# Score matmuls in blocks of 32 queries, and every loaded quad's probabilities turned by VectorE

## The chip, the cores and the metric

The kernel runs on one core of one Trainium2 chip. The metric is the device time of one execution in microseconds; the median of three runs of the kernel before is 609.25 us (608.87 to 609.41). TensorE has two clock levels, 1.2 and 2.4 GHz; in the profiled execution the granted clock is 1.00, that is 2.4 GHz, in every stretch.

## The reference

Attention over a window of fewer than 16 positions on either side, joined with one summary for each block of 32 positions, feeds a two-layer feed-forward part. Shapes: batch 4, 8 heads, 768 positions, 64 features a head; 3072 tokens of 512 features, hidden size 2048.

```
k_sum = k.reshape(B, H, 24, 32, D).max(axis=3)          # 24 summaries a sequence
v_sum = v.reshape(B, H, 24, 32, D).mean(axis=3)
scores_l = where(|i - j| < 16, q @ k.T / 8, -1e9)
scores_s = q @ k_sum.T / 8 + log(32)
a = softmax(concat([scores_l, scores_s]))               # divided by (sum + 1e-9)
x = (a @ concat([v, v_sum])) -> (3072, 512)
h = x @ w_in;  g = h * erf(softplus(h));  out = g @ w_out
```

## The kernel before

The tokens are worked in six chunks of 512 (NCH). Attention is worked in *quads*: one chunk for one pair of heads, four pairs, so 24 quads numbered 0 to 23. The feed-forward part is worked in 24 steps k, each a chunk and a quarter g of the hidden size. Step k computes h for its quarter (up to step 7 by `mm1`, L829; from step 8 by a scheme with seven products instead of eight, `products`, L870 to L879), applies softplus and erf on ScalarE, multiplies and splits the result into a high and a low part (`gsplit`, L971 to L983), and adds it into the output banks with three matmuls for one (`mm2`, L1000; the first two steps in one float32 matmul, L996).

Quads 0 to 3 are a special start: whole keys are loaded, masks are added by TensorE (L537), and scores go against windows of 96 keys and 24 summaries apart (L546). Quads 4 to 23 are *loaded* quads. `load_quad` loads 64 queries at a time against a window of 96 keys made on the host (`k_win`, 480 KB a quad); a copy puts the 24 key summaries behind each window (L259). `scores` (L546) makes, for each block of 64 queries and either head, one 64 x 64 matmul with 120 columns (96 keys, 24 summaries), into the PSUM banks pA and pB. A float32 matmul is recorded twice, so a quad has 32 records. `softmax` then adds the mask on VectorE (L637), takes the maximum (L642), has eight exponentials on ScalarE (L652) and normalizes on VectorE (L668).

The value product `av` (L711) wants the probabilities with keys on the partitions. There are two ways. Quads 4 to 11 are turned by TensorE: `transp` (L682) makes eight 128 x 120 transposes into pA and pB, and ScalarE copies the two banks into the tile ptr (L688). Quads 12 to 23 (DQ = 12) are turned by VectorE: `turn_blocks` transposes every 32 x 32 block of the 1024 columns (L569) into the tile tb, and sixteen moves of 32 x 256 or 24 x 256 (L259, by VectorE or ScalarE) bring the blocks to the right partitions of ptr. There is one tile for the probabilities (pr) and one for the turned ones (ptr).

All operations are put into a plan with what they read and write. The list ORDER names them by number in the order in which they are issued; a letter behind the number (d, a) gives VectorE or ScalarE where either can do it. Each engine works its own operations in this order, and all loads are issued from one queue (SP). Activation tables are loaded where the order of ScalarE's operations needs another one (L1269). Fixed numbers of idle matmuls fill TensorE's waits at the start (L1039). Weights are loaded and split into high and low parts on VectorE and ScalarE in the first 110 us; sums of weights for the later scheme are made in steps 5 to 7.

Of the kernel before, what the change touches and what calls it, by code (L numbers as in the profile page):

```python
# [25 lines left out]
NP = H // 2  # L26
# [7 lines left out]
NK = LW + NS  # L34
NCH = B * S // T
# [14 lines left out]
0 1 8 3 2 4 9 5 51 11 18 19 35 14 20 21 28 22 29 23 10 30 66 12 67 24 31 6 34 36 32 13 50 37 68 25 38 26 39 44 7 40 69 27d 225 70 45 33d 46 41 71 42  # L50
226 43d 105 72 47 48 107 49d 106a 52 108a 74 78 93d 94a 95 53 112 96 15 73 114 60 97 54 109 149 61 55 56 98 75 77 110a 16 113a 111 76 79 115a 57 62 17
58 59d 80 121 81 151 227a 123 63 174 82 64 87 83 116 65d 122 88 117d 89 119 84 118 173 125 99d 124a 130 100d 126a 251 90 101 132 152 91 102 133 85 92d
103 127 86d 104 136 128a 150 134 137a 120 129 135a 131 178 154a 153d 221 138 155 228a 141 139a 156 142 140 207 159a 144 160d 157 161 145 162 143 179a
158 146 163 229 243 165d 180a 166d 164 181 148 147 244 259 215 216 185 167 210 245 211 168 258 212 209 213 175 217 246 214d 247 218 182d 267 183d 219d
271 252 169d 170d 232 177 184 171 233 222 234 172 235 187d 220 264 248 189 230 249 186 188d 223 237 250 238 190 239 194d 191 240 231 176 265 193a 192
280 269 208 236a 320 254 224 273 241d 262 321 260d 195 275 261a 242 196 266 270 309 197 199d 253 200d 279 201 281 198 325 268 202 341 326 340 272 306
274 308 278 327 277 255 276 328 263 329 382 346 386 203d 204d 385 205 389 282d 330 284 256 310 257 331 206 288a 311 332 283a 307 312 290 314 313a 285
315 294a 336 342a 316 286 358 289d 344 343d 291 322 287 295a 292 317 333 323d 390 359 296 324 394 318a 337 300a 393 319 293 345 397 297 363 302 298
338 347 364 378 379 339 348 301a 374 400a 349 398 350 303 334 352 365 384 401d 304 375 353 354 366 351a 416 380a 355 367 335 299 388 392 356d 412 402
396 305 383 403 376 387 413 406a 368 407d 404 391 369 408 377 370 395 381a 357 360 405 424 361d 371 414 399 425 409 426 362 417d 427 430 418 410 419  # L60
411 431 420 372 449 421 415 422 450d 482 423a 451 481 428a 485 373 429 435 484 436 446 497 447 452 453 437 483 438 487 503 439 488 489 454 448d 432
# [12 lines left out]
875 892d 827a 927 826a 824d 828a 893 900 819a 818a 925 838 901a 897a 898 907a 823d 879 902 908 903a 904 909 914 905a 910 915 916 911 978 912 917d 920
932 913 979 981 918 957d 968 958d 961 971 919d 959 922 960 964 921 929 993 931 926 933 966 962 982 965 972 980 930 994d 934 970 973 996 974 969 975
935 995 936 976 987d 999 1082 997d 1001 988 1000d 1003 998 967a 1004 989a 937 1002d 1005 990 938 985d 1007 1006a 939 986 1009 1008a 983d 1011 1010a
940 984 1013 1012a 1015 1014 944a 950d 1017 942a 946d 1083 947a 948d 1019 943d 951a 1018 956a 954d 1021 952a 1084 1020 1023 992 1016 1027 955d 991
1024d 1022d 1028 1026 945d 949d 1029 941d 1025 953d 1030 1031 1087 1032 1033 1034 1086 1093 1035 1085 1036 1090 1037 1038 1070 1071 1066 1075 1063a
1073 1062d 1067 1039 1076 1077 1065 1040 1078 1069 1041 1079 1091d 1089 1080 1064 1092 1081 1096 1181 1094d 1072a 1098 1042 1095 1097a 1100 1074 1043
1101 1068 1099a 1102 1044 1088 1104 1103a 1045 1106 1105a 1108 1107a 1051d 1049a 1110 1047d 1109a 1057d 1059a 1060d 1112 1052a 1111 1046d 1048a 1114  # L80
1061d 1182 1053a 1055d 1054a 1116 1056d 1115 1058a 1113 1118 1183 1117 1120 1119a 1166 1122 1124 1050d 1125 1187 1126 1121a 1127 1185 1128 1129 1130
1123 1189 1131 1132 1184 1190d 1133 1191 1186 1134 1168 1135 1169 1164 1174 1172 1160 1165 1175 1161a 1136 1176 1159 1177 1137 1162 1138 1178 1163
1192 1179 1180 1167 1195 1281 1193d 1197 1188 1196a 1170a 1139 1194 1199 1173 1200 1265 1198a 1201 1140 1171d 1287 1203 1141 1202a 1205 1204a 1142
1207 1206a 1209 1208a 1148d 1150a 1147d 1211 1153a 1210 1156d 1144a 1213 1155d 1282 1152a 1157d 1291 1215 1149d 1214 1143a 1146d 1217 1283 1212 1219
1158d 1218d 1223 1292 1221 1372 1224 1285 1225 1145d 1216 1226 1154d 1227 1220d 1151d 1222 1228 1297 1229 1230 1231 1298d 1284 1286 1232 1299 1233
1268 1234 1267 1263 1274 1260a 1271 1258 1264 1235 1275 1289 1276 1261 1277 1236 1262 1237 1278 1259 1290 1279 1300 1280 1303 1269d 1388 1301d 1305
1270d 1304a 1302 1293 1307 1295 1272 1308 1294 1306a 1296 1309 1238 1266 1311 1310a 1313 1239 1288 1240 1312a 1315 1314a 1241 1317 1316a 1273 1319
1318 1247a 1321 1256d 1389 1320 1323 1322 1251d 1325 1255d 1390 1324 1327 1326d 1248d 1331 1329 1328d 1250d 1332 1242d 1330 1245d 1333 1244d 1254d
1392 1334 1253d 1252d 1257d 1335 1243d 1249d 1336 1246d 1337 1393 1402 1338 1339 1405 1391 1403a 1340 1404 1341 1374 1375 1342 1370 1381 1367a 1378
1371 1382 1368 1343 1383 1384 1366d 1344 1373 1345 1385 1386 1369 1396d 1387 1398d 1397 1408 1406d 1491 1399 1410 1376d 1409a 1407 1394a 1412 1377a  # L90
1379 1346 1413 1400d 1411a 1395 1347 1414 1401 1348 1416 1415a 1349 1418 1417a 1420 1419a 1353d 1364a 1422 1357d 1421a 1356d 1355a 1361d 1424 1365a
1423 1358d 1354a 1426 1380 1350d 1363a 1352d 1492 1360a 1428 1359d 1427 1351a 1425 1430 1493 1429 1432 1431a 1362d 1434 1436 1433d 1437 1438 1435 1439
1440 1495 1441 1442 1443 1496 1497 1444 1494 1445 1500 1498a 1446 1477 1447 1478 1475 1484 1481 1476 1471d 1485 1448 1486 1474 1487 1449 1472d 1450
1499 1488 1489 1473 1490 1503 1501d 1584 1505 1479a 1451 1504a 1502 1480a 1507 1482 1452 1508 1506a 1453 1509 1454 1511 1510a 1513 1512a 1470d 1459a
1515 1461d 1514a 1467d 1463a 1468d 1517 1460a 1516d 1483 1456d 1457a 1519 1518 1458a 1465a 1521 1520 1585 1462a 1523 1469a 1522 1464a 1525 1455a 1524
# [70 lines left out]
def block_attention_mlp(ctx: ExitStack, tc: tile.TileContext, q_t, k_nat, k_win, v_tok, v_nat, v_win, w_in, w_out, out):  # L166
# [42 lines left out]
    for m in (mask_h, mask_sb):  # L209
        nc.scalar.copy(m, band.unsqueeze(1).to_broadcast([128, 7, NK]))  # L210
# [1101 lines left out]
```

## Time and profile before

| | |
|---|---|
| Median of three runs | 609.25 us |
| The profiled execution, its span | 609.45 us, 607.7 us |
| TensorE matmuls, weight loads | 601.8 us (99%), 500.7 us (82%) |
| VectorE, ScalarE, GpSimd | 472.3 us (78%), 457.6 us (75%), 4.7 us (1%) |
| Moved by the queues | 153.35 MB, 252 GB/s in the mean |

The span runs from the first to the last instruction; the rest of the execution's time lies around it. Busy time is the time in which an engine has an instruction under way. Matmuls overlap: the next begins before the one ahead has ended, so the time that one costs is read from start to start, not from its duration.

### The profile page before, as it was taken

Reading aid. Unit: us, or ns where it says so; the run is one execution under the profiler, and the core shown is the slowest. Engines: PE = TensorE matmul, PEld = TensorE weight load, DVE = VectorE, ACT = ScalarE, POOL = GpSimd, SP = SyncE. Lnnn points to the kernel's source line nnn. Section 1 sums busy time; section 2 is a strip of 40 time slices with the busy share of each in tenths; the row PEclk is TensorE's granted clock in tenths of the full one; section 3 lists DMA queues with packets and bytes.
Section 4 is the critical chain, followed back from the end, with each engine's and each line's share of the span. In section 5 each row is a group of like instructions: output and inputs, shape, how many; then the busy total and the mean of one; then the engine's idle time right before and its main releaser. Section 6 shows DMA issues by size and latency. Waiting matters only on the chain.

```text
span 607.7 us, 11862 instructions
## 1 busy us (share of the span) xinstructions
PE 601.8 (99%) x4624; PEld 500.7 (82%) x4624; DVE 472.3 (78%) x810; ACT 457.6 (75%) x925; POOL 4.7 (1%) x29
## 2 busy tenths in 40 slices
PE   9999999999999999999999999999999999999997
PEld 4677476888888889889889889899898898888886
DVE  4899899757799999979799968669778677546452
ACT  5879799866969798977987787887886884652550
POOL 3000000000000000000000000000000000000000
PEclk9999999999999999999999999999999999999999
DMA  8999866463757778898777786766786664665611
GB/s 315 377 397 420 311 213 243 161 230 106 273 180 267 266 304 297 328 347 294 292 258 263 276 269 232 286 215 230 282 291 234 243 201 154 246 239 190 225 70 69
DMA packets 37610, 153.35 MB, mean 252 GB/s; under 512 B 3956, under 2 KB 9396, under 8 KB 27060
## 3 DMA queue, kind: packets, MB, share of 16 engines
q1 hardware_dynamic: 36980, 152.09, 69.3%
q8 instruction: 36, 0.59, 0.4%
q10 hardware_dynamic: 576, 0.52, 0.2%
q14 instruction: 18, 0.15, 0.1%
HBM read 127.27 MB, written 23.07 MB: 247 GB/s over the span
## 4 chain that ended last, share of the span: by engine, by line
PE 96%; DMA 3%; ACT 0%; SPq 0%; issue 0%; DVE 0%
PE ops L1000 40%; PE h L829 15%; PE hb L879 11%; PE ha L879 11%; PE ops L996 5%; PE px L711 4%; PE pA L546 3%; PE hb L870 2%; DMA vwf<-vsum 2%; PE hb L873 1%; DMA vt<-v_tok 1%; PE vs L482 1%; PE pA L682 1%; PE pB L682 1%; PE vt L440 0%; PE pB L546 0%
## 5 line engine op out<-in xcount | busy, mean ns | idle before, releaser
L1000 PE MATMUL ops<-w,gh 128*128 128x512 f32 x704 | 229.2, 394 | 0.0
L1000 PEld LDWEIGHTS ops<-w,gh 128*128 128x128 f32 x704 | 132.5, 188 | 28.6 <-issue 0.8
L1000 PE MATMUL ops<-w,gl 128*128 128x512 f32 x352 | 137.4, 390 | 0.0
L1269 ACT ACT_TABLE_LOAD x87 | 111.6, 1283 | 1.5
L976 DVE TENSOR_TENSOR hc<-wt,hc 128x1024 f32<-128x1024 f32 x44 | 52.7, 1221 | 62.5 <-ACT wt L964 62.4
L829 PE MATMUL h<-x,w 128*128 128x512 f32 x384 | 96.9, 399 | 0.0
L829 PEld LDWEIGHTS h<-x,w 128*128 128x128 f32 x384 | 70.7, 188 | 17.0 <-issue 2.3
L1000 PEld LDWEIGHTS ops<-w,gl 128*128 128x128 f32 x352 | 66.2, 188 | 12.4
L652 ACT ACTIVATE pr<-pr,stats 128x120 f32<-128x120 f32 x160 | 61.0, 383 | 14.1 <-DVE stats L661 13.8
L259 ACT COPY hc<-hb 128x256 f32<-128x256 f32 x68 | 25.1, 370 | 48.0 <-PE hb L873 17.9
L983 DVE TENSOR_TENSOR gl<-hc,gh 128x1024 fp32r<-128x1024 f32 x44 | 53.7, 1221 | 0.9 <-ACT gh L259 0.3
L964 ACT ACTIVATE wt<-wt 128x1024 f32<-128x1024 f32 x48 | 49.5, 1056 | 0.4
L879 PE MATMUL hb<-w,ws 128*128 128x256 f32 x288 | 42.3, 283 | 0.0
L879 PEld LDWEIGHTS hb<-w,ws 128*128 128x128 f32 x288 | 38.0, 192 | 0.1
L958 ACT ACTIVATE wt<-hc 128x1024 f32<-128x1024 f32 x32 | 32.5, 1053 | 7.2 <-DVE hc L259 4.1
L259 ACT COPY ptr<-tb 32x256 f32<-32x256 f32 (+1 forms) x84 | 33.9, 404 | 4.2 <-DVE tb L569 3.0
L259 DVE COPY ptr<-tb 32x256 f32<-32x256 f32 (+1 forms) x108 | 30.8, 285 | 2.2
L652 ACT ACTIVATION_READ_ACCUMULATOR pr<-pr,stats 128x1 f32 x160 | 30.0, 188 | 0.0
L996 PE MATMUL ops<-a32s,gw 128*128 128x512 f32 x64 | 29.1, 593 | 0.0
L879 PE MATMUL ha<-w,ws 128*128 128x256 f32 x192 | 28.2, 283 | 0.0
L879 PE MATMUL ha<-x,ws 128*128 128x256 f32 x192 | 28.1, 283 | 0.0
L259 DVE CAST gh<-hc 128x1024 fp32r<-128x1024 f32 x28 | 19.3, 688 | 10.0 <-PE ops L1000 9.8
(173 smaller groups left out, 966.7 us busy)
## 6 DMA issues: line engine op xcount, KB each, us to landing
w<-dr SPq DMA_DIRECT2D x36, 1024.0 KB
ws<-ds SPq DMA_DIRECT2D x30, 1024.0 KB
vw<-v_win SPq DMA_DIRECT2D x20, 512.0 KB
kw<-k_win SPq DMA_DIRECT2D x20, 480.0 KB
dr<-w SPq DMA_DIRECT2D x8, 1024.0 KB
ds<-ws SPq DMA_DIRECT2D x8, 1024.0 KB
rw<-w_in SPq DMA_DIRECT2D x8, 1023.8 KB
rw<-w_out SPq DMA_DIRECT2D x8, 1023.8 KB
```

The costliest lines, as they stand in the source:

```text
L259: e.copy(o, i) if e is nc.scalar else e.tensor_copy(o, i)
L652: nc.scalar.activation(s["pr"][:, j], s["pr"][:, j] if qd >= MQ else s["sc"][j // NI][:, i * NK:(i + 1) * NK], AF.Exp, scale=0.125, bias=s ...
L711: nc.tensor.matmul(shape, lhsT=s["vw"][0:NK, j, r], rhs=y, start=True, stop=True)
L829: nc.tensor.matmul(hs[k, f][:, 0:T], lhsT=w[m], rhs=xt[ch, cc][x], start=(cc == 0 and n == 0), stop=(cc == 3 and n == 2))
L879: nc.tensor.matmul(shape, lhsT=w[m], rhs=y[l], start=first and c == 0 and i == 0, stop=c == 1 and i == 2, skip_group_check=True)
L958: nc.scalar.activation(wt[k, n], hc[k, n], AF.Softplus)
L964: act(0.96, lambda n=n: nc.scalar.activation(wt[k, n], wt[k, n], AF.Erf, scale=-1.0 if k < SOFT else 1.0), [s], [s], table=("sig",), after ...
L976: e.tensor_tensor(hc[k, n], wt.pop((k, n)), hc[k, n], op=ALU.mult)
L983: e.tensor_tensor(gs[k, n][1], hc.pop((k, n)), f32(gs[k, n][0]), op=ALU.subtract)
L996: nc.tensor.matmul(os_[ch, t], lhsT=x[0][:, i % 2, t * 128:(t + 1) * 128], rhs=w32["o", g, i // 2][:, i % 2], start=first, stop=last)
L1000: nc.tensor.matmul(os_[ch, t], lhsT=x[y][:, i % 2, t * 128:(t + 1) * 128], rhs=w[m], start=first and n == 0, stop=last and n == 2)
L1269: nc.scalar.preload_act_table_set(sets[loaded])
```

## The change

Scores of loaded quads go in blocks of 32 queries. A block needs 64 keys (`LQ`), and with 24 summaries 88 columns (`NQK`). The host makes 16 windows of 64 keys for a quad, 704 KB. There are 32 matmuls of 64 x 32 with 88 columns for a quad, twice recorded each. Mask, maximum, exponentials and normalization go over 88 columns for each block where there were 120. The probability tile has 96 columns a block (`COLS`), which are three 32 x 32 blocks.

All quads from 4 on are turned by VectorE; `transp` and its copies are gone. For quads 4 to 11 the transposition is done in place in pr, for the others into tb. There are twelve moves for a quad: two of 32 keys, whose place depends on whether the block of 32 queries is even or odd in its 64, and one of 24 summaries. The value product still goes over 120 rows; the 32 rows that a block doesn't have are set to zero once, after quad 3, by `clear_turned` on VectorE.

The float32 mask (now 88 wide) is made by GpSimd after all its other preparations; ScalarE makes only the half-width mask of the first quads, 480 columns instead of 840. The list ORDER is made anew for the whole kernel: 2372 operations, before 2331. In it the query and key loads of quad 4 come behind the three broadcasts of the value sums (vwf<-vsum); before they stood ahead of them. Of the 96 moves of quads 4 to 11 it gives 46 to VectorE and 50 to ScalarE. Of the 32 copies of h out of the banks in steps 0 to 7 (`hout`) it gives 25 to ScalarE, before 18. ScalarE's operations stand so that the activation table is loaded 90 times, before 87; up to the value product of quad 11 it is 32 times, before 36.

```diff
-            keys(lambda r, j: [(0, s["kw"][r, j])])
+            for b in range(QB):
+                i, r = divmod(b, 4)
+                for a in range(2):
+                    x = slice(64 * a, 64 * a + 64)
+                    nc.tensor.matmul(s["sc"][a][32 * r:32 * r + 32, i * NQK:(i + 1) * NQK], lhsT=s["qb"][x, 32 * b:32 * b + 32], rhs=s["kw"][x, b], start=True, stop=True, skip_group_check=True)
...
+    def clear_turned():
+
+        def go(e):
+            t = sb([128, 4, 2 * NI, 32], F32, "ptr", "pt")
+            turned_to.append(t)
+            for z, r in ((slice(64, 96), 0), (slice(0, 32), 1)):
+                o = t[z].rearrange("k (j r) n q -> k r j (n q)", r=2)[:, r]
+                x = zeros[z].bitcast(F32)[:, 0:1].unsqueeze(2).to_broadcast([32, 2, 256])
+                copy(e, o, x)
+        cleared.append(on({"DVE": 0.845}, go, [], [f"pt{r}3" for r in range(4)]))
...
-            s["tb"] = sb([128, 4, 2 * NI, 32], F32, "tb", "x6")
-            e.transpose(s["tb"].rearrange("q c n k -> q n c k"), prob.rearrange("q n (c k) -> q n c k", c=4))
+            if qd >= DQ:
+                s["tb"] = sb([128, 3, 2 * NI, 32], F32, "tb", "x6")
+            else:
+                s["tb"] = prob.rearrange("q n (c k) -> q c n k", c=3)
+            e.transpose(s["tb"].rearrange("q c n k -> q n c k"), prob.rearrange("q n (c k) -> q n c k", c=3))
...
-            n = min(32, NK - 32 * c)
-            copy(e, s["pt"][32 * c:32 * c + n, r], s["tb"][32 * r:32 * r + n, c])
+            n, at = (32, c + r % 2) if c < 2 else (NS, 3)
+            copy(e, t[32 * at:32 * at + n, r], s["tb"][32 * r:32 * r + n, c])
...
-    def transp(qd):
...
+    nc.gpsimd.tensor_copy(mask_sb, band_of(NQK, LQ, 32, "gl1").to_broadcast([128, 7, NQK]))
...
-    k_win[..., :LW] = windows(k).transpose(0, 2, 3, 5, 1, 4).reshape(NCH, NP, 128, NB, LW)
+    k_win[..., :LQ] = windows(k, 32, LQ).transpose(0, 2, 3, 5, 1, 4).reshape(NCH, NP, 128, QB, LQ)
```

## Rows read from the trace of the kernel before

**Rows 1.** The page's first part: engine, busy us, share of the span, instructions.
```profile
PE 601.8 (99%) x4624; PEld 500.7 (82%) x4624; DVE 472.3 (78%) x810; ACT 457.6 (75%) x925; POOL 4.7 (1%) x29
```
**Rows 2.** The page's fourth part: the chain that ended last, by engine.
```profile
PE 96%; DMA 3%; ACT 0%; SPq 0%; issue 0%; DVE 0%
```
**Rows 3.** Waits of TensorE: who waited for whom, us, times, longest.
```profile
PE idle L1039 <- DVE zeros L192: 1.1, 1, 1.1
PE h L546 <- DMA qf<-q_t: 0.9, 1, 0.9
PE vs L482 <- DMA vt<-v_tok: 0.3, 1, 0.3
PE px L711 <- DMA vwf<-vsum: 0.2, 1, 0.2
```
**Rows 4.** Timeline of TensorE around a set of transposes: start, us, operation, count.
```profile
150.33 0.60 PE L682 MATMUL pA<-ident,pr 128*120 128x128 f32 x4
...
151.12 0.48 PE L829 MATMUL h<-x,w 128*128 128x512 f32 x1
```
**Rows 5.** Groups by line of TensorE: busy us, mean ns, idle before.
```profile
L682 PE MATMUL pA<-ident,pr 128*120 128x128 f32 x32 | 4.8, 272 | 0.0
```
**Rows 6.** Timeline of TensorE: a set of scores (quad 10).
```profile
155.39 0.31 PE L546 MATMUL pA<-kw,qb 64*64 64x120 f32 x1
...
155.55 0.26 PE L546 MATMUL pA<-kw,qb 64*64 64x120 f32 x1
...
155.57 0.26 PE L546 MATMUL pB<-kw,qb 64*64 64x120 f32 x1
...
156.16 0.26 PE L546 MATMUL pA<-kw,qb 64*64 64x120 f32 x1
...
156.37 0.98 PE L829 MATMUL h<-x,w 128*128 128x512 f32 x3
```
**Rows 7.** Timeline of TensorE: scores of quad 0, 96 and 24 columns.
```profile
6.57 0.24 PE L546 MATMUL pA<-kf,qf 64*64 64x96 f32 x1
...
6.65 0.24 PE L546 MATMUL pA<-kf,qf 64*64 64x96 f32 x1
...
6.88 0.23 PE L546 MATMUL pA<-ksum,qf 64*64 64x24 f32 x2
...
7.06 0.22 PE L546 MATMUL pA<-ksum,qf 64*64 64x24 f32 x2
```
**Rows 8.** Stretches: length, busy us of PE, PEld, DVE, ACT, POOL; clock, DMA share, GB/s.
```profile
30.00:105.00 75.00, 75.00 (x480) 50.41 (x479) 70.75 (x114) 66.16 (x121) 0.00 (x0) 1.00 0.82 316
225.00:608.00 383.00, 379.19 (x2871) 335.86 (x2867) 281.99 (x505) 271.96 (x542) 0.00 (x0) 1.00 0.68 241
30.00:225.00 195.00, 195.00 (x1345) 147.73 (x1345) 170.85 (x258) 164.59 (x306) 0.00 (x0) 1.00 0.70 259
165.00:210.00 45.00, 45.00 (x314) 36.64 (x313) 44.28 (x65) 36.03 (x61) 0.00 (x0) 1.00 0.68 237
```
**Rows 9.** Groups by line and shape of VectorE: busy us, mean ns, idle before.
```profile
L668 DVE TENSOR_TENSOR pr<-pr,stats 128x960 f32<-128x960 f32 x20 | 23.1, 1155 | 0.4
L259 DVE COPY ptr<-tb 32x256 f32<-32x256 f32 x78 | 22.1, 284 | 1.6
L569 DVE STREAM_TRANSPOSE tb<-pr 128x1024 f32<-128x1024 f32 x12 | 14.9, 1243 | 0.3
L770 DVE TENSOR_TENSOR x<-px,x 128x512 fp32r<-128x512 f32 x8 | 5.5, 683 | 0.1
```
**Rows 10.** Groups by line and shape of ScalarE.
```profile
L1269 ACT ACT_TABLE_LOAD x87 | 111.6, 1283 | 1.5
L259 ACT COPY ptr<-tb 32x256 f32<-32x256 f32 x66 | 26.6, 404 | 3.2 <-DVE tb L569 2.3
L688 ACT COPY ptr<-pA 120x512 f32<-120x512 f32 x8 | 4.7, 582 | 3.3 <-PE pA L682 2.0 <-PE px L711 1.3
```
**Rows 11.** DMA issues by line: count, KB of one.
```profile
kw<-k_win SPq DMA_DIRECT2D x20, 480.0 KB
```

More of the change, by code (lines that the diff above doesn't have):

```diff
@@ L34 @@
 NK = LW + NS
+QB = T // 32
+LQ = 64
+NQK = LQ + NS
+COLS = NQK + 8
 NCH = B * S // T
@@ L54 @@
[L54 to L61, printed above, removed]
@@ L198, in block_attention_mlp, with band_of @@
     ident_h, ones, cst = small[:, 0:128], small[:, 128:256], small[:, 256:256 + NI * NS]
-    mask_sb = sb([128, 7, NK], F32, "mask_sb")
-    mask_h = sb([128, 1024], BF16, "mask_h")[:, 0:7 * NK].rearrange("q (i c) -> q i c", i=7)
+    mask_sb = sb([128, 7, NQK], F32, "mask_sb")
+    mask_h = sb([128, 1024], BF16, "mask_h")[:, 0:NI * NK].rearrange("q (i c) -> q i c", i=NI)
     nc.scalar.copy(ident_h, ident)
-    band = sb([128, NK], F32, "band", "gl0")
-    nc.gpsimd.memset(band[:, 0:LW], 0.0)
-    nc.gpsimd.memset(band[:, LW:NK], 8.0 * math.log(32.0))
-    for c in range(2):
-        m = band[64 * c:64 * c + 64, 0:LW]
-        nc.gpsimd.affine_select(out=m, in_=m, pattern=[[1, LW]], compare_op=ALU.is_ge, fill=-8e9, base=-1, channel_multiplier=-1)
-        nc.gpsimd.affine_select(out=m, in_=m, pattern=[[-1, LW]], compare_op=ALU.is_ge, fill=-8e9, base=31, channel_multiplier=1)
-    for m in (mask_h, mask_sb):
-        nc.scalar.copy(m, band.unsqueeze(1).to_broadcast([128, 7, NK]))
+    def band_of(n, w, size, tag):
+        band = sb([128, n], F32, "band", tag)[:, 0:n]
+        nc.gpsimd.memset(band[:, 0:w], 0.0)
+        nc.gpsimd.memset(band[:, w:n], 8.0 * math.log(32.0))
+        for c in range(128 // size):
+            x = band[size * c:size * c + size, 0:w]
+            nc.gpsimd.affine_select(out=x, in_=x, pattern=[[1, w]], compare_op=ALU.is_ge, fill=-8e9, base=-1, channel_multiplier=-1)
+            nc.gpsimd.affine_select(out=x, in_=x, pattern=[[-1, w]], compare_op=ALU.is_ge, fill=-8e9, base=31, channel_multiplier=1)
+        return band.unsqueeze(1)
+    nc.scalar.copy(mask_h, band_of(NK, LW, 64, "gl0").to_broadcast([128, NI, NK]))
     nc.gpsimd.memset(ones, 1.0)
@@ L218, in block_attention_mlp @@
         rest -= c
[L219 to L222 removed]
+    nc.gpsimd.memset(mask_h[0:64, 0, 0:16], -8e9)
     tops = sb([128, 2, 512], U32, "top", "x6")
@@ L242, in block_attention_mlp @@
         nc.gpsimd.memset(pick[32 * i:32 * i + 32, 116 + i:117 + i], 1.0 / 32.0)
+    nc.gpsimd.tensor_copy(mask_sb, band_of(NQK, LQ, 32, "gl1").to_broadcast([128, 7, NQK]))
+    for i in (0, 5):
+        nc.gpsimd.memset(mask_sb[0:32, i, 0:16], -8e9)
+    nc.gpsimd.memset(mask_sb[96:128, 4, LQ - 16:LQ], -8e9)
     P = Plan()
@@ L501, in go_k @@
         def go_k():
-            s["kw"] = sb([128, NB, NK], F32, "kw")
+            s["kw"] = sb([128, QB, NQK], F32, "kw")
             nc.sync.dma_start(out=s["kw"], in_=k_win[ch, p])
         dma(262, go_q, w=["qb"])
-        dma(465, go_k, w=["kw"])
+        dma(680, go_k, w=["kw"])
         for b, js in seqs:
-            n = js.stop - js.start
-            on({"DVE": 0.08 + 0.025 * n, "ACT": 0.1 + 0.02 * n}, lambda e, b=b, js=js, n=n: copy(e, s["kw"][:, js, LW:NK], ksum[:, b % 2, p:p + 1, :].to_broadcast([128, n, NS])),
+            n = 2 * (js.stop - js.start)
+            js = slice(2 * js.start, 2 * js.stop)
+            on({"DVE": 0.154 + 0.0122 * n, "ACT": 0.196 + 0.0198 * n}, lambda e, b=b, js=js, n=n: copy(e, s["kw"][:, js, LQ:NQK], ksum[:, b % 2, p:p + 1, :].to_broadcast([128, n, NS])),
                [f"ksum{b % 2}{p}"], ["kw"])
@@ L533, in mask @@
             s["sc"] = [tiles[n] for n in banks]
-            m0 = mask_at[qd // NP % 3]
             for sc in s["sc"] if qd < MQ else []:
-                nc.tensor.matmul(sc[:, 0:NI * NK], lhsT=ident_h, rhs=mask_h[:, m0:m0 + NI], start=True, stop=False, skip_group_check=True)
+                nc.tensor.matmul(sc[:, 0:NI * NK], lhsT=ident_h, rhs=mask_h, start=True, stop=False, skip_group_check=True)
                 nc.tensor.matmul(sc[:, 0:NI * NK].rearrange("q (i c) -> q i c", i=NI)[:, :, LW:NK], lhsT=ones, rhs=cst.rearrange("o (i c) -> o i c", i=NI), start=False, stop=False, skip_group_check=True)
@@ L545, in keys @@
                         n += j // 2 * NK
-                        nc.tensor.matmul(s["sc"][a][o, n:n + rhs.shape[-1]], lhsT=s["qb"][r, 64 * j:64 * j + 64], rhs=rhs, start=qd >= MQ, stop=True, skip_group_check=True)
+                        nc.tensor.matmul(s["sc"][a][o, n:n + rhs.shape[-1]], lhsT=s["qb"][r, 64 * j:64 * j + 64], rhs=rhs, start=False, stop=True, skip_group_check=True)
         def near(r, j):
@@ L551, in near, with blocks @@
             return [(0, kn[r, k0:k0 + LW])] if j else [(0, kn[r, 0:16]), (16, kn[r, 0:LW - 16])]
-        def both():
+        def blocks():
             mask()
-            keys(lambda r, j: [(0, s["kw"][r, j])])
+            for b in range(QB):
[3 more added lines that the diff above has]
+                    nc.tensor.matmul(s["sc"][a][32 * r:32 * r + 32, i * NQK:(i + 1) * NQK], lhsT=s["qb"][x, 32 * b:32 * b + 32], rhs=s["kw"][x, b], start=True, stop=True, skip_group_check=True)
         if qd >= NP:
-            pe(1.06 if qd >= MQ else 1.64, both, ["qb", "kw"] + (["mh"] if qd < MQ else []), banks)
+            pe(0.86, blocks, ["qb", "kw"], banks)
         else:
@@ L561, in scores @@
             pe(0.5, lambda: keys(lambda r, j: [(LW, ksum[r, 0, qd])]), [f"qf{qd}", f"ksum0{qd}"], banks)
+    turned_to, cleared = [], []
+    def clear_turned():
[7 more added lines that the diff above has]
+        cleared.append(on({"DVE": 0.845}, go, [], [f"pt{r}3" for r in range(4)]))
     def turn_blocks(qd):
         s = st[qd]
+        own = "x6" if qd >= DQ else "pr"
         def go(e):
-            s["tb"] = sb([128, 4, 2 * NI, 32], F32, "tb", "x6")
-            e.transpose(s["tb"].rearrange("q c n k -> q n c k"), prob.rearrange("q n (c k) -> q n c k", c=4))
-        def move(e, c, r):
-            if "pt" not in s:
-                s["pt"] = sb([128, 4, 2 * NI, 32], F32, "ptr", "pt")
-                s["at"] = lambda a, j: s["pt"][0:NK, 2 * (j % 2):2 * (j % 2) + 2, NI * a + j // 2]
-            n = min(32, NK - 32 * c)
-            copy(e, s["pt"][32 * c:32 * c + n, r], s["tb"][32 * r:32 * r + n, c])
-        on({"DVE": 1.17}, go, ["pr"], ["x6"])
+            if qd >= DQ:
[3 more added lines that the diff above has]
+            e.transpose(s["tb"].rearrange("q c n k -> q n c k"), prob.rearrange("q n (c k) -> q n c k", c=3))
+        def move(e, c, r):
+            t = turned_to[0]
+            s["at"] = lambda a, j: t[0:NK, 2 * (j % 2):2 * (j % 2) + 2, NI * a + j // 2]
+            n, at = (32, c + r % 2) if c < 2 else (NS, 3)
+            copy(e, t[32 * at:32 * at + n, r], s["tb"][32 * r:32 * r + n, c])
+        on({"DVE": 0.981}, go, ["pr"], [own])
         for r in range(4):
-            for c in range(4):
-                on({"ACT": 0.41, "DVE": 0.3}, lambda e, c=c, r=r: move(e, c, r), ["x6"], [f"pt{r}{c}"])
+            for c in range(3):
+                on({"ACT": 0.41, "DVE": 0.3}, lambda e, c=c, r=r: move(e, c, r), [own], [f"pt{r}{c}"], after=cleared)
     def softmax_first(qd, banks):
```

221 lines of the change are left out of this document (98 added, 123 removed).

## Prediction

> **What bounds the kernel now.** I read the page's busy table first. TensorE is busy in 601.8 of 607.7 us [rows 1], but its matmuls overlap, so that alone doesn't make it the bound. The chain of waits does: 96% of it is TensorE [rows 2]. The waits of TensorE then say how often it stood for another engine: four times, 2.5 us in sum [rows 3], and from 30 to 225 us it is busy throughout [rows 8]. So the end moves by what TensorE no longer issues, minus what it must newly wait for. VectorE and ScalarE set nothing now, but I come back to how close they are.
>
> The profiled execution took 609.45 us, 1.75 more than its span; the median of the runs is 609.25. I sum against 609.45 and take off 0.2 at the end.
>
> **Transposes off TensorE.** Quads 4 to 11 (a quad: one pair of heads of one 512-token chunk) are turned by eight transposes each. In the timeline the first starts at 150.33 and the next work at 151.12 [rows 4]: 0.79 us, and the trace has 32 of them on either bank, eight quads [rows 5]. 8 x 0.79 = 6.3 us less issue, all of it on the path.
>
> **Scores in blocks of 32 queries.** Twenty loaded quads. Before, a set is 32 matmul records, in eight groups of four that run beside each other: the first starts at 155.39, the second group at 155.55, the last at 156.16, the next work at 156.37 [rows 6]. That is 0.98 us. After, there are twice as many records, each with 88 columns instead of 120 and 32 stationary columns, and the diff writes them so that eight different positions of the array (two row halves, four column quarters) follow each other: again eight groups, of eight. What does a group cost? At 120 columns the pitch is 0.10 (0.61 over six), at 96 columns, in the first quads, 0.08 (6.57 to 6.65) [rows 6, 7]: some 0.85 ns a column, so 0.075 at 88, if a group of eight goes like one of four. The set: 0.13 to the second group, 6 x 0.075, 0.21 to the next work = 0.79, a gain of 0.19, over 20 quads 3.8 us. No row shows eight positions at once. Better bound: the last wait shrinks with the columns too, 0.22 a quad, 4.4 us. Worse bound by the nearest rows: with 24 columns, where the columns hardly count, four records still take 0.06 us (6.88 to 7.06 is three groups) [rows 7], 15 ns a record; 64 records at that price are 0.96 us against 0.82 for the old 32, so 0.14 lost a quad, 2.8 us. I take 3.8: inside a group the records start 0.01 us apart or less (the first and the fourth of the second group stand at 155.55 and 155.57) [rows 6], so eight fit into 0.075.
>
> The Trainium skill speaks against it: "TensorE: Matmul & The Clock Gate", section "Wait — 56ns, not 53.3ns?", says that starts of matmuls never lie under about 25 ns apart, however few the columns. By that rule a set would take 64 x 25 = 1.6 us, an estimate from the page. The 24-column rows, at 15 ns a record [rows 7], stand against it as a limit across positions of the array.
>
> **What this puts on VectorE and ScalarE.** Stretch 30 to 225 us, where quads 4 to 11 are worked: VectorE is busy 170.9 of 195, ScalarE 164.6 [rows 8]. Changes there:
> VectorE's cost a column is (1155 - 683) / (960 - 512) = 1.05 ns [rows 9]. Normalization has a row, 960 columns; mask addition (two halves of 480) and maximum go over the same number. Each loses 256 columns, 0.27 us: 0.80 less a quad. The turn, 1.24 us at 1024 columns, is 0.97 at 768 [rows 9], new for these quads. So +0.17 a quad, 1.4 us for eight. Then twelve moves a quad of 284 ns on VectorE or 404 on ScalarE [rows 9, 10]; the new order marks 46 of the 96 for VectorE: 13.1 us, and 20.2 on ScalarE for its 50. The same order gives ScalarE seven more of the 512-column copies out of the first products (25 of 32, before 18): 7 x 0.68 = 4.8 us off VectorE, 7 x 0.58 = 4.1 onto ScalarE. The two copies of 582 ns behind the TensorE transposes fall: 8 x 1.16 = 9.3 off ScalarE. Table loads, counted along the two orders up to the value product of the last of these quads: 32, before 36, so 4 x 1.28 = 5.1 off ScalarE [rows 10]; in the whole list 90, before 87, the rest in a stretch with room.
> VectorE 170.9 + 1.4 + 13.1 - 4.8 = 180.6; ScalarE 164.6 + 20.2 + 4.1 - 9.3 - 5.1 = 174.5. Together 355.1.
> TensorE itself wants to be quicker there by 6.3 + 9 x 0.19 = 8.0: 187 us, in which the two engines have 374. That is 95% of both. Here lies the price. What share can they hold? Between 30 and 105 they held (70.8 + 66.2) / 150 = 91% with TensorE never waiting; between 165 and 210 VectorE alone 98% [rows 8]. At 91% the stretch lasts 195 us and nothing of the 8.0 is left (7.5 to 8 lost); at 98% nothing is lost. The 91% was no limit, as nobody waited, so the truth lies between: I take 3.5 us of new waits, and keep 0 and 8 as ends. What is queued behind a late VectorE is the product of the gate (hc, gl) that the second matmul reads, so TensorE stands at L1000 or L829.
>
> After 225 us the same sums go the other way: twelve quads lose 0.80 + 0.27 us on VectorE and four of sixteen moves each, and the two engines have room (282 and 272 of 383) [rows 8]. There TensorE keeps its 11 x 0.19.
>
> **Transfers.** A key window grows from 480 KB [rows 11] to 704 (16 x 88 columns), 4.6 MB over the kernel. Between 30 and 105 us the queues are 82% busy at 316 GB/s [rows 8]: 0.7 us more for each of the three quads loaded there. The new order takes quad 4's query and key loads behind the broadcast of the value sums, which is itself on the chain early on; the weights behind them come up to 0.7 us later each. I cost it at 0, since no wait of TensorE names a key's or a weight's transfer [rows 3], and keep +1.
>
> **Masks, the cleared tile.** The small mask copy on ScalarE falls short, the other is made by GpSimd last, and VectorE clears the tile after quad 3 with two writes of 512 columns, at most 2 x 0.68 us by the nearest row [rows 9]. The first scores wait for a query transfer, 0.9 us [rows 3], not for the mask. I take nothing, between -0.9 (that wait gone) and +1.4 (the writes in full, if VectorE's next output is awaited).
>
> **Sum.** 609.45 - 6.3 - 3.8 + 3.5 - 0.2 = 602.6 us.
>
> **Rivals.**
> *Full cover.* VectorE and ScalarE hold 95 to 98%, TensorE never waits: 609.25 - 10.1 = 599.1; with the better bound of the scores 598.5. For it: 98% was held for 45 us. Against: that was one engine, not both.
> *The early gain is eaten.* They hold 91 to 92%: 8.0 lost; 609.25 - 10.1 + 8 = 607.2.
> *Slower: VectorE and ScalarE become the bound up to 225 us.* The turn and its moves sit between normalization and the value product, in one probability buffer and one turned buffer, so each engine waits for the other. It decides where the joint share falls under 355.1 / (2 x 197) = 90%; at their present mean of (170.9 + 164.6) / 390 = 86% the stretch takes 206 us, 11 more than now, and with 2.1 gained later the time is 618; at 88%, 614. Against: 86% is a share that nobody asked more of.
> *Each small matmul has a price of its own.* At 15 ns a record 2.8 lost instead of 3.8 gained: 602.6 + 6.6 = 609.2. At the 25.6 ns that a record took on average in the old groups (0.61 / 24, whatever sets it), the set lasts 0.82 longer: +16.4, some 623 [rows 6]. The 24-column rows leave the second little chance [rows 7]. The page of the Trainium skill named above would have it come about so.
>
> **How the numbers follow.** Forecast (600.5 to 605): 0.48. Full cover: 0.20. Early gain eaten (605 to 608): 0.12. Price a matmul at 15 ns: 0.08; at 25.6: 0.02. Engines become the bound: 0.10. What a measurement here can tell from no change is about 0.2%, 1.2 us. Faster: 0.48 + 0.20 + 0.12 = 0.80; same: 0.08; slower: 0.12. The range leaves out the two slow cases and a little at the fast end: 598.7 to 608.7.
>
> **What would show it.** Right: no transposes of pr on TensorE after 40 us; a score set, first start to next work, near 0.79 us; VectorE at 95% or more and ScalarE over 90% from 30 to 220 us; new waits of TensorE for VectorE or ScalarE of 2 to 5 us in sum, all before 225; 158 MB moved. Wrong: a set of 0.98 or more (the groups of eight don't run beside each other); waits over 8 us; waits for kw or w transfers, which I cost at nothing; or TensorE idle after 225.

## The result and the profile after

The kernel after takes 599.44 us in the median (598.99 to 599.89), the kernel before, run beside it, 609.06 (608.45 to 609.41): 0.9843 of it, with a 95% interval of 0.9826 to 0.9860. That is 9.6 us faster. The forecast was 602.6, with a range of 598.7 to 608.7. The time lies in the range, but below the band of 600.5 to 605 in which the forecast stood: it came out as in the rival of full cover, 599.1.

The profiled execution took 599.2 us with a span of 597.2, 10.5 less than the span before. Busy time by engine in the kernel after, as in [rows 1]:

```profile
PE 592.2 (99%) x5200; PEld 493.2 (83%) x5200; DVE 477.4 (80%) x851; ACT 458.5 (77%) x931; POOL 7.2 (1%) x38
```

VectorE has 5.1 us more work, ScalarE 0.9 more, and TensorE's busy time fell by 9.6. The chain of waits by engine, as in [rows 2], still goes through TensorE:

```profile
PE 95%; ACT 2%; DMA 1%; DVE 1%; issue 0%; ACTq 0%
```

All waits of TensorE in the kernel after (who waited for whom, us in sum, times, longest), as in [rows 3]:

```profile
PE idle L1037 <- DVE zeros L197: 1.1, 1, 1.1
PE h L827 <- DVE x L727: 0.2, 1, 0.2
```

Here the forecast is refuted. There is one new wait for another engine, 0.2 us where I had put 3.5; the three waits for transfers of [rows 3] (qf, vt, vwf, 1.4 us) are not there. That they are gone is no gain of the change that can be counted on: such waits at the start come and go from one execution to the next. All waits of TensorE in an experiment further down, the kernel before with the maximum of quads 4 to 11 taken twice, whose first 30 us are the same program:

```profile
PE idle L1040 <- DVE zeros L192: 1.1, 1, 1.1
PE hb L880 <- ACT hc L259: 0.2, 1, 0.2
```

In that execution no transfer was waited for either. In the groups by line no transposes of pr are left on TensorE. The bytes came as worked out:

```profile
DMA packets 37616, 158.03 MB, mean 265 GB/s; under 512 B 3956, under 2 KB 9396, under 8 KB 27060
```

A score set in TensorE's timeline (quad 16; start, us, operation), to stand against [rows 6]; of each group of eight records the first is shown, then the last record and the next work:

```profile
305.31 0.26 PE L567 MATMUL pA<-kw,qb 64*32 64x88 f32 x1
...
305.41 0.24 PE L567 MATMUL pA<-kw,qb 64*32 64x88 f32 x1
...
305.49 0.24 PE L567 MATMUL pA<-kw,qb 64*32 64x88 f32 x1
...
305.56 0.24 PE L567 MATMUL pA<-kw,qb 64*32 64x88 f32 x1
...
305.64 0.24 PE L567 MATMUL pA<-kw,qb 64*32 64x88 f32 x1
305.68 0.26 PE L567 MATMUL pB<-kw,qb 64*32 64x88 f32 x1
...
306.03 0.24 PE L567 MATMUL pB<-kw,qb 64*32 64x88 f32 x1
306.19 0.39 PE L709 MATMUL px<-ptr,vw 120*64 120x64 f32 x6
```

The second group follows the first by 0.10 us, the next ones by 0.076, as forecast, up to 32 records. Then the order breaks: the record that opens the fifth group stands alone, the next comes 0.04 later, and from there on the records run in a more even row. The fifth group takes 0.14 us in place of 0.076, the two behind it 0.08 and 0.09. From first start to next work the set takes 0.88 us. I had 0.79; before it was 0.98.

Stretches of the kernel after, as in [rows 8] (length, then busy us of TensorE, its weight loads, VectorE, ScalarE, GpSimd; granted clock, DMA share, GB/s); quads 4 to 11 are now done by 221 us:

```profile
30.00:105.00 75.00, 75.00 (x624) 50.51 (x623) 72.16 (x125) 71.46 (x135) 0.00 (x0) 1.00 0.86 334
30.00:221.00 191.00, 190.77 (x1590) 144.96 (x1589) 181.80 (x303) 179.93 (x351) 0.00 (x0) 1.00 0.76 283
221.00:600.00 379.00, 372.69 (x3187) 330.12 (x3186) 274.25 (x497) 258.06 (x502) 0.00 (x0) 1.00 0.69 248
```

From 30 to 221 us VectorE is busy 95.2% and ScalarE 94.2%, and TensorE all but never waits. I had forecast 180.6 and 174.5 us of work for the two; VectorE came within 1.2 us, ScalarE does 5.4 more.

VectorE's groups by line and shape (busy us, mean ns, idle before), to stand against [rows 9]:

```profile
L681 DVE TENSOR_TENSOR pr<-pr,stats 128x704 f32<-128x704 f32 x20 | 17.8, 888 | 0.4
L669 DVE TENSOR_REDUCE stats<-pr 128x8 f32<-128x704 f32 x20 | 17.7, 884 | 0.4
L598 DVE STREAM_TRANSPOSE tb<-pr 128x768 f32<-128x768 f32 x12 | 11.7, 978 | 0.4
L598 DVE STREAM_TRANSPOSE pr<-pr 128x768 f32<-128x768 f32 x8 | 7.8, 974 | 0.1
```

Normalization fell from 1155 ns to 888, the forecast 0.27 us; the turn takes 0.978 and 0.974 us, forecast 0.97.

### The profile page after: what moved, and what is told of

The parts are those of the page before. It is cut to its first block, busy times and chain, and to the rows that moved or that the text cites. A ratio compares the mean times of both kernels' runs of the same rounds, so it can differ in the third digit from the quotient of the medians.

```text
span 597.2 us, 13035 instructions
## 1 busy us (share of the span) xinstructions
PE 592.2 (99%) x5200; PEld 493.2 (83%) x5200; DVE 477.4 (80%) x851; ACT 458.5 (77%) x931; POOL 7.2 (1%) x38
## 4 chain that ended last, share of the span: by engine, by line
PE 95%; ACT 2%; DMA 1%; DVE 1%; issue 0%; ACTq 0%
PE ops L998 39%; PE h L827 14%; PE hb L877 12%; PE ha L877 12%; PE ops L994 5%; PE px L709 4%; PE hb L868 2%; PE pA L567 2%; DMA kw<-k_win 1%; PE hb L871 1%; PE pB L567 1%; PE idle L1037 1%; ACT pr L674 0%; PE h L554 0%; ACT prf L624 0%; PE vs L490 0%
## 5 line engine op out<-in xcount | busy, mean ns | idle before, releaser
L998 PE MATMUL ops<-w,gh 128*128 128x512 f32 x704 | 244.1, 394 | 0.0
L827 PE MATMUL h<-x,w 128*128 128x512 f32 x384 | 99.6, 404 | 0.2 <-DVE x L727 0.2
L674 ACT ACTIVATE pr<-pr,stats 128x88 f32<-128x88 f32 x160 | 56.7, 356 | 3.8 <-DVE stats L684 3.5
L267 ACT COPY hc<-hb 128x256 f32<-128x256 f32 x47 | 17.4, 371 | 48.4 <-PE hb L871 17.5
L956 ACT ACTIVATE wt<-hc 128x1024 f32<-128x1024 f32 x32 | 33.7, 1059 | 18.9 <-DVE hc L267 10.7
L877 PE MATMUL hb<-w,ws 128*128 128x256 f32 x288 | 41.1, 282 | 0.0
L267 ACT COPY ptr<-tb 32x256 f32<-32x256 f32 (+1 forms) x71 | 28.6, 403 | 10.9 <-DVE tb L598 9.9
L267 DVE COPY hc<-hb 128x256 f32<-128x256 f32 x49 | 20.4, 420 | 12.4 <-PE hb L871 6.6
L877 PEld LDWEIGHTS ha<-x,w 128*128 128x128 f32 x192 | 26.6, 190 | 2.0
L877 PE MATMUL ha<-x,w 128*128 128x256 f32 x192 | 27.9, 282 | 0.0
```

The source lines that it names most:

```text
L267: e.copy(o, i) if e is nc.scalar else e.tensor_copy(o, i)
L674: nc.scalar.activation(pr[:, j], pr[:, j], AF.Exp, scale=0.125, bias=s["mx"][:, j:j + 1], accum_out=sm[:, j:j + 1])
L827: nc.tensor.matmul(hs[k, f][:, 0:T], lhsT=w[m], rhs=xt[ch, cc][x], start=(cc == 0 and n == 0), stop=(cc == 3 and n == 2))
L877: nc.tensor.matmul(shape, lhsT=w[m], rhs=y[l], start=first and c == 0 and i == 0, stop=c == 1 and i == 2, skip_group_check=True)
L956: nc.scalar.activation(wt[k, n], hc[k, n], AF.Softplus)
L998: nc.tensor.matmul(os_[ch, t], lhsT=x[y][:, i % 2, t * 128:(t + 1) * 128], rhs=w[m], start=first and n == 0, stop=last and n == 2)
```

## The experiments

Each kernel ran beside the kernel before on one chip. Differences to the kernel after are worked out from the two ratios, times 609.1 us, and each is uncertain by 1 to 2 us. Several kernels repeat work whose result is overwritten with the same values, or add work that nothing reads; one leaves out idle matmuls, none leaves out work that the result needs.

**Scores twice.** In the kernel after, the matmuls of each loaded quad's set are issued twice in a row:

```diff
-            for b in range(QB):
+            for b in [*range(QB), *range(QB)]:
```

> The changed kernel with every score matmul of a loaded quad issued twice in the same set (128 records instead of 64). In the changed kernel's trace the first 32 records of a set go in groups of eight 0.076 us apart, the other 32 take longer, and the set 0.886 us. Theory S1 (the columns set the pace, the loss is a fixed one at the set's end): the added 64 records are eight more groups, 8 x 0.076 = 0.61 us a quad, 12.2 over 20 quads: 611.6. Theory S2 (what lies beyond the first 32 records is held by the rate at which TensorE is fed, about 0.022 us a record as the second half shows from 305.31 to 306.03): 64 x 0.022 = 1.4 us a quad, 28 us: 628.

Measured: 624.26 us, 1.0255 of before (1.0233 to 1.0276), 25 us more than after. The first record and the next work of a set in this kernel's TensorE timeline:

```profile
315.21 0.26 PE L567 MATMUL pA<-kw,qb 64*32 64x88 f32 x1
...
316.80 0.39 PE L709 MATMUL px<-ptr,vw 120*64 120x64 f32 x6
```

The set went from 0.886 us (the usual length over the 20 sets) to 1.59: 0.705 for 64 more records, 11 ns each, 14.1 us in all. So the pace behind the first 32 records stays near 11 ns a record, where the undisturbed groups go at 9.4: 0.09 us a set more than the first theory's 0.61, and half of the second theory's 1.4. The second theory's 0.022 us a record was a misreading: the stretch from 305.64 to 306.03 holds 32 records, 13 ns each. Of the other 11 us some 8 are waits of TensorE that I had not foreseen, and some 2 go to the granted clock, which was 0.997 over this execution. The largest of the waits:

```profile
PE pB L567 <- issue: 2.8, 1, 2.8
PE px L709 <- issue: 2.2, 2, 1.1
PE ops L998 <- ACT wt L962: 1.3, 1, 1.3
PE idle L1037 <- DVE zeros L197: 1.1, 1, 1.1
PE ops L998 <- issue: 0.8, 1, 0.8
```

"Issue" is time in which the engine waited for nothing that the profile shows. The kernel after has none on TensorE. So the price of a score set is read from its length, not from this kernel's time.

**32 more matmuls of 24 columns.** They stand ahead of each set and write into places that the set itself overwrites; the loops are those of the set:

```diff
...
+                    nc.tensor.matmul(s["sc"][a][32 * r:32 * r + 32, i * NQK + LQ:(i + 1) * NQK], lhsT=s["qb"][x, 32 * b:32 * b + 32], rhs=s["kw"][x, b, LQ:NQK], start=True, stop=True, skip_group_check=True)
```

> The changed kernel with 32 more matmuls (64 records) ahead of each set, of 24 columns each, overwritten by the set itself. S1 (columns): 24 columns are 0.02 us a group of eight, some 0.16 to 0.3 us a quad, 3 to 6 us in all: 603 to 605. S2 (rate of feeding): as much as with 88 columns, 20 to 28 us: 620 to 628. Between them, at the 0.015 us a record of the first quads' 24-column matmuls: 0.96 us a quad, 19 us: 619.

Measured: 620.33 us, 1.0191 (1.0174 to 1.0208), 21 us more than after. The first record and the next work of a set:

```profile
314.38 0.21 PE L567 MATMUL pA<-kw,qb 64*32 64x24 f32 x1
...
315.79 0.39 PE L714 MATMUL px<-ptr,vw 120*64 120x64 f32 x6
```

1.41 us, 0.52 more than after, for 64 records: 8 ns a record of 24 columns, where 88 columns cost 11, both as means over the added records. Neither theory meets it: the whole kernel's time falls into the second theory's range, but half of the 21 us is not the sets. The columns count for little, so there is a price of its own for each record; but it is 8 ns, half of the 15 that I took from [rows 7], where only four positions of the array alternate. Again waits on nothing shown stand beside it, 7.4 us in sum, and a granted clock of 0.996, some 2 us. The largest of the waits:

```profile
PE pB L572 <- issue: 3.2, 1, 3.2
PE px L714 <- issue: 2.9, 2, 1.6
```

**The transposes back.** Eight transposes of the identity per quad for quads 4 to 11, at the place where `transp` stood, without the copies behind them; nothing reads what they write:

```diff
+            if NP <= qd < DQ:
+                for i in range(NB):
+                    nc.tensor.transpose(xo[0:NK, i % NI * 128:(i % NI + 1) * 128], ident[:, 0:NK], ident)
```

> The changed kernel with eight 128x120 transposes of the identity matrix put back on TensorE ahead of each value product of quads 4 to 11; nothing else reads them. Theory A (TensorE's issue is the only bound): 8 x 0.79 to 0.85 = 6.3 to 6.8 us slower, 605.7 to 606.2. Rival B (VectorE and ScalarE, at 95% of 30 to 221 us, hold the stretch): part of it hides behind their work, 599.4 to 603.

Measured: 605.99 us, 0.9956 (0.9939 to 0.9973), 6.9 more than after (6.6 by the medians); expected by the theory that TensorE's issue is the path 8 x 0.79 = 6.3. Its one wait of TensorE over the whole span:

```profile
PE idle L1040 <- DVE zeros L197: 1.1, 1, 1.1
```

The one wait is that of every kernel's start. What TensorE issues moved the end at full price, as theory A has it; no other engine was holding the stretch.

**Wide blocks, turned by VectorE.** The kernel after with the scores in blocks of 64 queries and 120 columns, as before: softmax over 960 columns, the turn over 1024, sixteen moves in the twelve places of the order.

```diff
-            for b in range(QB):
-                i, r = divmod(b, 4)
+            for j in range(NB):
...
-            n, at = (32, c + r % 2) if c < 2 else (NS, 3)
-            copy(e, t[32 * at:32 * at + n, r], s["tb"][32 * r:32 * r + n, c])
+            for m in (c,) if c < 2 else (2, 3):
+                n = min(32, NK - 32 * m)
+                copy(e, t[32 * m:32 * m + n, r], s["tb"][32 * r:32 * r + n, m])
```

> The changed kernel with the blocks of 64 queries back (120 columns, 32 score records a quad, mask, maximum and normalization over 960, four 32-column blocks to turn, sixteen moves in the places of twelve), but all loaded quads turned by VectorE and in the same order. In 30 to 221 us VectorE gets about 8 x 1.07 + 16 x 0.28 = 13 us more (181.8 to 195 of 191) and ScalarE 7 more (180 to 187). Theory B (95% is near the end of what both hold): TensorE must wait 4 to 15 us, 605 to 616. Rival A (there is room, only TensorE's issue counts): scores 0.095 slower a quad, 1.9 us: 601.3.

Measured: 614.61 us, 1.0093 (1.0072 to 1.0113): slower than the kernel before, and 15 us slower than after, in theory B's range. The sets are back at 0.981 us, which is 1.9 of the 15. The waits of TensorE rise from 1.3 to 10.2 us, nearly all for the two other engines; some 4 us stand in no row of the waits and are not assigned. The stretch of quads 4 to 11:

```profile
30.00:221.00 191.00, 184.34 (x1234) 137.48 (x1233) 183.75 (x302) 178.20 (x347) 0.00 (x0) 1.00 0.69 254
```

TensorE loses 6.7 us here, and the stretch is not done at 221: the value product of quad 11 begins at 228.1 us, 9.9 later than after. Its largest waits of TensorE but that of the start, all for ScalarE's copies and VectorE:

```profile
PE px L708 <- ACT hc L267: 1.7, 2, 1.1
PE hb L876 <- ACT hc L267: 1.1, 3, 0.6
...
PE h L826 <- DVE stats L683: 1.0, 1, 1.0
```

In this order, turning all quads by VectorE pays only with the narrow blocks, which free 0.80 us of softmax and four moves a quad for it. One reservation: the order was laid for the narrow durations, and one made for the wide ones might lose less; that was not tried.

**Where the edge of VectorE lies, early.** The maximum of quads 4 to 11 is taken twice, as below, then in another kernel four times:

```diff
-            e.tensor_reduce(s["mx"], pr, op=ALU.max, axis=AX.X)
+            for _ in range(2 if NP <= qd < DQ else 1):
+                e.tensor_reduce(s["mx"], pr, op=ALU.max, axis=AX.X)
```

> The changed kernel with the maximum of quads 4 to 11 taken twice on VectorE (0.8 us from start to start, 8 times: 6.4 us more in 30 to 221 us, where it is busy 181.8 of 191). Theory B (VectorE is at its end there): TensorE waits for most of it, 603 to 606. Rival A (outputs lie ready well ahead of TensorE): 599.4 to 600.5.

> The same with the maximum taken four times: 19 us more on VectorE in 30 to 221 us, 201 of 191, which can't be hidden there. Theory B: 12 to 19 us slower, 611 to 618. Rival A: the work that isn't needed before 221 us slips behind it, less than 8 us slower, under 607.

Measured: twice 603.36 us, 0.9901 (0.9883 to 0.9918), 3.5 more than after, in theory B's range; four times 623.34 us (619.49 to 626.33), 1.0228 (1.0180 to 1.0276), 23 more and beyond both theories. I had priced a repeat at 0.80 us, the step from a maximum to the next instruction. The repeats cost more. In VectorE's timeline of a kernel below, which takes four for quads 12 to 23, four of them begin at 294.93 and the next instruction at 298.61:

```profile
294.93 3.65 DVE L670 TENSOR_REDUCE stats<-pr 128x8 f32<-128x704 f32 x4
298.61 0.17 DVE L685 TENSOR_SCALAR stats<-stats 128x8 f32<-128x8 f32 x1
```

3.65 us less the 0.885 of one is 0.92 for each repeat. So 7.4 us were added by the first kernel, of which 3.5 show, and 22.1 by the second. Its profiled execution, the fastest of the four, has a span 20.3 us longer than after; 12.7 of them are waits of TensorE. The stretch in the first kernel, then in the second:

```profile
30.00:221.00 191.00, 187.25 (x1542) 140.72 (x1541) 183.64 (x304) 175.64 (x345) 0.00 (x0) 1.00 0.74 278
```

```profile
30.00:221.00 191.00, 178.08 (x1474) 132.05 (x1473) 182.77 (x298) 160.53 (x313) 0.00 (x0) 0.96 0.67 251
```

VectorE gets to 183.6 and 182.8 of 191 us, 183.8 with the wide blocks: about 96% in three kernels that all make TensorE wait. That is its edge in this stretch and order, and the kernel after stands at 95.2%. Four times, the mean granted clock was 0.96: behind four of the waits TensorE ran at 1.2 GHz for a while. One of these, as a stretch with long waits and the stretch behind it:

```profile
94.00:98.00 4.00, 1.50 (x81) 1.00 (x76) 3.90 (x7) 2.41 (x5) 0.00 (x0) 0.97 0.43 135
98.00:101.00 3.00, 3.00 (x13) 1.83 (x6) 3.00 (x6) 2.94 (x16) 0.00 (x0) 0.50 0.35 58
```

A clock of 0.96 over 191 us is worth some 7 us. So of the 22.1 us added about 13 show as waits, and the clock makes up the rest of the price.

**The same in the kernel before.** The maximum of quads 4 to 11 twice:

```diff
-                e.tensor_reduce(s["mx"], s["pr"], op=ALU.max, axis=AX.X)
+                for _ in range(2 if NP <= qd < DQ else 1):
+                    e.tensor_reduce(s["mx"], s["pr"], op=ALU.max, axis=AX.X)
```

> The kernel before, with the maximum of quads 4 to 11 taken twice (1.06 us from start to start, 8 times: 8.5 us more on VectorE in 30 to 225 us, where it is busy 170.9 of 195). Theory L (idle share is room): 88% goes to 92%, 0 to 1 us slower. Theory O (each engine works its list in order, and what counts is how far ahead of TensorE's need the list has been laid): about the share that the changed kernel lost, 61%: 5 us slower, 614.

Measured: 609.64 us, 1.0013 (1.0003 to 1.0022), 0.8 more than before, as theory L has it. A repeat over 960 columns takes 1.19 us by this kernel's timeline, so 9.5 us of work on VectorE cost 0.8. The stretch:

```profile
30.00:221.00 191.00, 191.00 (x1303) 144.20 (x1302) 173.33 (x260) 159.17 (x301) 0.00 (x0) 1.00 0.70 260
```

At 91% of VectorE TensorE still never stands idle there. The kernel before had this room, and the change used most of it up.

**Whether the idle share after 225 us is room.** After 221 us VectorE is busy 72% in the kernel after. The maximum of quads 12 to 23 is taken four times and, in another kernel, twice; in the kernel before, four times:

```diff
+            for _ in range(4 if qd >= DQ else 1):
+                e.tensor_reduce(s["mx"], pr, op=ALU.max, axis=AX.X)
```

> The changed kernel with the maximum of quads 12 to 23 taken four times: 12 x 3 x 0.8 = 29 us more on VectorE after 221 us, where it is busy 274 of 376. Theory A and B alike: room for it, 599.4 to 601. Otherwise the place in the chain (scores, softmax, turn, value product) counts and not the load: 1 to 2 us a quad, 610 to 625.

> The changed kernel with the maximum of quads 12 to 23 taken twice (0.8 us, 12 times: 9.6 us). Taken four times it cost 25.4 of 28.8 us. Theory O with no room at all: a third, 8.5 us, 608. With some room a step (28.8 - 25.4 = 3.4 us over 12 quads, 0.28 each): 9.6 - 3.4 = 6.2 us, 605.6. Theory L: 599.4.

> The kernel before, with the maximum of quads 12 to 23 taken four times (12 x 3 x 1.06 = 38 us more on VectorE after 225 us, busy 282 of 383). Theory L: room for it, 609 to 611. Theory O: 1.5 to 3 us a quad show, as in the changed kernel, 627 to 645.

Measured: after with four 624.83 us, 1.0264 (1.0240 to 1.0288), 26 more than after, of 36 x 0.92 = 33 added; with two 602.02 us, 0.9885 (0.9866 to 0.9904), 2.6 more, of 11 added; before with four 649.05 us, 1.0661 (1.0638 to 1.0685), 40 more than before, of 36 x 1.19 = 43 added. I had taken the idle share for room and had expected next to nothing of four in the kernel after; then, for two and for the kernel before, values that were all missed as well. The granted clock has a part in it: 0.997 in the kernel after with four, some 2 us, and 0.986 in the kernel before with four, some 9 us. The stretch with four in the kernel after, and the largest waits of TensorE in it:

```profile
221.00:600.00 379.00, 361.69 (x3114) 317.65 (x3113) 296.33 (x521) 250.94 (x495) 0.00 (x0) 1.00 0.68 247
```

```profile
PE ha L878 <- DVE x L769: 3.6, 2, 2.0
PE ha L878 <- DVE traw L782: 3.0, 2, 2.2
PE ha L878 <- DVE traw L772: 2.7, 2, 2.0
```

VectorE is busy 78%, and TensorE waits for it. What VectorE's idle time is made of shows in the kernel after, in the waits of VectorE over the whole span, of which these are the three largest:

```profile
DVE pr L665 <- PE pB L567: 14.4, 7, 3.4
DVE hc L974 <- ACT wt L962: 13.2, 13, 2.7
DVE hc L938 <- PE hb L877: 9.1, 11, 3.2
```

It stands because the instruction at its head awaits the scores, ScalarE or the first products; whatever is behind in its list stands too. When the scores are there, the softmax chain has a length of its own, and TensorE comes back for x after it. How much is due to the list's order and how much to the length of this chain was not separated. From two to four, 22 us were added and 23 showed. With two, 8.4 of 11 were hidden, 0.70 us a quad; with four 7.5 of 33, 0.62 a quad. So a step in the kernel after has some 0.6 to 0.8 us to spare, and beyond that nearly everything shows.

**Fewer idle matmuls.** At 20.4 us the kernel after issues eight matmuls of zeros, which nothing reads. They are left out:

```diff
-FILL = {66: 6, 69: 2, 109: 1, 79: 8}
+FILL = {66: 6, 69: 2, 109: 1}
```

> The changed kernel without the eight idle matmuls ahead of quad 3's scores (20.40 to 22.23 us in its trace, 1.8 us). If they now stand on TensorE's path (no wait of TensorE is left in the first 30 us but the first, 1.1): up to 1.8 us faster, 597.6 to 598.9. If the softmax of the first quads on ScalarE sets the start, TensorE waits where it filled: 599.4, and the clock may fall for a stretch: up to 601.

Measured: 598.87 us (598.31 to 600.71), 0.9836 (0.9815 to 0.9858): no difference to 0.9843 that can be told. Its waits of TensorE:

```profile
PE idle L1037 <- DVE zeros L197: 1.1, 1, 1.1
PE h L554 <- issue: 0.7, 1, 0.7
PE px L709 <- DMA vwf<-vsum: 0.5, 2, 0.3
```

1.2 us of new waits stand in the place of the eight, among them the one for the value sums of [rows 3], though in a single execution such waits at the start can be chance. The kernel before has the same eight matmuls, so they are no part of the gain; and leaving them out gave nothing.

## Why the prediction was right, and where it was not

Of its signs of being right three came: no transposes of pr, VectorE at 95.2% and ScalarE at 94.2%, 158 MB. Two did not: the set takes 0.886 us, not 0.79, and the new waits are 0.2 us, not 2 to 5. Of its signs of being wrong none came.

**TensorE's issue sets the end: right.** Read from the chain and the waits [rows 2, 3], and shown by the transposes put back.

**Transposes, 6.3 us: right, a little low.** 6.6 to 6.9 by the experiment. I had priced all eight places by one; in the trace of before five take 0.79 us from start to next work, one 0.87 and two 0.96, 6.8 in sum.

**Scores, 3.8 us: half of it.** The sets shrank by 0.095 us, not 0.19: 1.9 us in all. The step that failed is "so eight fit into 0.075": they do in the first four groups, after which the fifth takes 0.065 more, the next two 0.01 to 0.02 more each, and from the start of the last group to the next work it is 0.24 us where I had 0.21. What breaks the row after 32 records is not settled. The rule of the Trainium skill that I weighed ("TensorE: Matmul & The Clock Gate", section "Wait — 56ns, not 53.3ns?"), no starts under about 25 ns, does not hold here across positions of the array: a record more costs 8 ns with 24 columns and 11 with 88, a matmul of two records 16 and 22. So neither a price of 15 ns nor one of 25.6 came, and 24-column rows in four positions were a bad measure for eight.

**New waits, 3.5 us: wrong, 0.2 came.** The failed step is "so the truth lies between: I take 3.5 us of new waits". I read shares that I had seen, 91% and 98%, as if the limit had to lie halfway, though nobody waited at either. The work of VectorE was sized well (181.8 against 180.6), that of ScalarE 5.4 us too low (179.9 against 174.5), and the edge, by three kernels, is at about 96% of VectorE. The kernel after stops just short of it. As nobody had waited at either share, neither bounded anything, and full cover deserved more than the 0.20 that I gave it; but it was a near thing, since 7.4 us more of VectorE's work cost 3.5, and nothing that I had read beforehand told on which side of the edge 95% lies. The two other rivals of this kind, an early gain that is eaten and engines that become the bound, did not come; what they describe is the wide blocks and the repeated maxima, one step further on.

**Transfers and masks at nothing: right in the main.** No wait names a transfer of kw or w; the queues' share from 30 to 105 us rose from 0.82 to 0.86. The query wait of 0.9 us, the better bound that I had kept, is absent here as in an execution of the kernel before with the maximum taken twice, so it is not to be booked as a gain. The price of the cleared tile was not measured apart.

**"The two engines have room" after 225 us: no harm here, but false as a reason.** Their work went down there, so nothing was asked of the room; 2.8 us a quad more on VectorE (three repeats of the maximum) cost 26 us.

The sum by the traces: transposes 6.8, scores 1.9, together 8.7 us. By the medians the gain is 9.6 us, with an interval of 8.5 to 10.6, so 0.9 us are not assigned. Between the two profiled executions the span fell by 10.5; of the 1.8 us left there, 1.2 are the waits (from 2.5 to 1.3), which the start of an execution can have or not.

Of the 3.2 us between the forecast and the time, 1.4 are what two errors of size leave that work against each other: 1.9 us too much gain for the scores and 3.3 us too much for the waits. The transposes gave 0.5 more, and 1.3 us stay open. That the rival of full cover was met within 0.3 us is luck in part: it had the scores at 3.8.

## What to carry to other kernels

Where one engine's issue is the path, an operation on it is worth its step from start to start, at full price; on the others, work was free up to an edge, and beyond it cost a part of what was added at first, and then nearly all of it. A busy share doesn't show the edge: VectorE held 95% here without cost, and in another stretch, raised from 72% to 78%, it cost 26 us. The waits suggest why: its list stands in order behind what it awaits. Double one operation of the engine in question, and price the doubling from the timeline, before you believe in room. And before you book a vanished wait as a gain, look whether another execution of the same code has it.

## What the runs showed of the hardware

- Of score matmuls that go round eight positions of the array, 64 records more in a set cost 8 ns each with 24 columns and 11 ns each with 88. The first 32 records of a set with 88 columns go at 9.4 ns each in the mean; the eight behind them take 0.065 us more than eight before, and from there on the pace is near 11 ns. The cause is open.
- Two kernels with more matmuls on TensorE have 5.8 and 7.4 us of waits for nothing that the profile shows, up to 3.2 us at once; the kernel after has none. The instruction queue moved 0.84 MB in either, 0.67 in the kernel after, and the four longest of these waits in either kernel end 2.2 to 2.7 us after a packet of that queue starts, while such packets lie some 12 us apart in the mean. That this is the cause was not shown: no run varied it alone.
- A maximum over 704 columns delays the next instruction on VectorE by 0.80 us where that one works on other tiles, and by 0.92 where it reads the result or writes the same tile; over 960 columns 1.06 to 1.07 and 1.19.
- TensorE's clock fell to 1.2 GHz for a while behind long waits: from 98 to 101 us the granted clock was 0.50, behind 4 us in which TensorE was busy for 1.5 (the maximum four times, quads 4 to 11).
